# Loading the output weights four rows per partition, with the heads split on VectorE, in a decode attention kernel

## The chip, the cores and the metric

The kernel runs on one core of one Trainium2 chip. The metric is device time of one execution, in microseconds. The granted TensorE clock was 0.78 to 0.80. PE is TensorE, PEld its weight loads, DVE is VectorE, ACT is ScalarE, POOL is GpSimd, and SP is the engine that issues the loads. In the lines of the profile a trailing q (SPq, PEq, DVEq) means the part of an engine that issues instructions. A packet is one record of a DMA engine's work; the core has 16 DMA engines.

## The reference, cut to what matters

```python
def _A_ref(x, k_cache, v_cache, wq, wo):        # x 1x1x448, Hq 16, Hkv 8, Sk 65536, Dh 256
    q = (x @ wq).reshape(B, Sq, Hq, Dh).transpose(0, 2, 1, 3)
    k = jnp.repeat(k_cache, rep, axis=1); v = jnp.repeat(v_cache, rep, axis=1)
    p = _softmax(jnp.einsum("bhqd,bhkd->bhqk", q, k) * (Dh ** -0.5))
    o = jnp.einsum("bhqk,bhkd->bhqd", p, v)
    return o.transpose(0, 2, 1, 3).reshape(B, Sq, Hq * Dh) @ wo       # wo: 4096 x 448
# ... B: a small token-mixing MLP; the result is g * a + (1 - g) * b
```

One query attends over 65536 keys. K and V are 268 MB each, all in bf16, and each byte is read once. The 16 query heads share 8 K/V heads, so the work falls into 8 groups of two heads, and each group needs its own 512 rows of `wo` (448 KB).

## The kernel before

Each group is cut into six chunks (`SIZES`), so there are 48 chunks. SP issues the loads in program order. There are two K buffers and one V buffer. The V of chunk `i` and the K of chunk `i+2` wait for the same event (`s_vf`): DVE has drained the P·V sums of chunk `i-1` from PSUM.

```python
def load_k(i):
    ...
    if i >= 2: sp.wait_ge(s_vf, i - 1)
    sp.dma_start(out=kbuf[i % 2][:, 0:n], in_=kv_src(A_k_cache, i)).then_inc(s_k[i % 2], 16)
def load_v(i):
    ...
    if i >= 1: sp.wait_ge(s_vf, i + 1)
    sp.dma_start(out=vbuf[:, 0:n], in_=kv_src(A_v_cache, i)).then_inc(s_v, 16)
def load_wo(g):                       # two pieces of 1792 B per partition
    if g >= 1: sp.wait_ge(s_oo, g)
    sp.dma_start(out=wo[:].rearrange("p r c n -> p r (c n)"),
        in_=A_wo[g*512:(g+1)*512, :].rearrange("(r p c) n -> p r (c n)", r=2, c=2)).then_inc(s_wo, 16)
# ...
for i in range(1, total - 1):
    load_v(i)
    if i % PER == 1 and PER < i < total - PER: load_wo(i // PER)
    if i + 2 < total: load_k(i + 2)
```

In the first chunk of each group but the first, a "group boundary", the kernel finishes the group before it. There are seven of these. On DVE:

```python
drain_pv(False).then_inc(s_vf, 1)               # releases V and K
dve.memset(tick[:], 0.0).then_inc(s_g, 1)       # lets PE turn the output
take(dve, s_e); dve.transpose(out=pT[:], in_=p_t[:]).then_inc(s_pt, 1)
take(dve, s_o); rden_gate(o_ps[:, 0, 2:4])      # 1/denominator times gate
take(dve, s_wo, 16); heads().then_inc(s_ot, 1)
```

PE turns `og` into a column per head with four small fp32 matmuls (`o_turn(4)`), then multiplies by `wo` with four matmuls of 448 columns. The last group has its own tail after the loop, and its weights come in two separate loads.

The softmax here doesn't subtract the row's maximum and nothing guards it: scores larger than these inputs give would overflow.

Of the kernel before, what the change touches and what calls it, by code (L numbers as in the profile page):

```python
# [8 lines left out]
FP32 = mybir.dt.float32  # L9
BF16 = mybir.dt.bfloat16  # L10
ACT = mybir.ActivationFunctionType
ALU = mybir.AluOpType
AXIS = mybir.AxisListType
# [3 lines left out]
DH = 256  # L17
# [77 lines left out]
def kernel(  # L95
# [16 lines left out]
    D = A_x.shape[-1]  # L112
# [14 lines left out]
    const = ctx.enter_context(tc.tile_pool(name="const", bufs=1))  # L127
# [8 lines left out]
    misc = psum.tile([128, 512], FP32, name="misc")  # L136
    den_ps = psum.tile([128, 512], FP32, name="den_ps")
    acc = psum.tile([128, 512], FP32, name="acc")
# [11 lines left out]
    mask = const.tile([128, 8, 32], FP32, name="mask")  # L150
    one_b = const.tile([128, 128], BF16, name="one_b")
    one_f = const.tile([1, 128], FP32, name="one_f")
    col_f = const.tile([128, 1], FP32, name="col_f")
# [4 lines left out]
    gate = const.tile([128, 2], FP32, name="gate")  # L158
# [17 lines left out]
    dmul = const.tile([128, PER], FP32, name="dmul")  # L176
    dsum = const.tile([128, 1], FP32, name="dsum")
    rden = const.tile([128, 2], FP32, name="rden")
    og = const.tile([128, 2 * DH], FP32, name="og")
    tick = const.tile([1, 1], FP32, name="tick")  # L180
    q_row = const.tile([128, 512], BF16, name="q_row")
    oT = const.tile([128, 4], BF16, name="oT")
    wo = const.tile([128, 2, 2, D], BF16, name="wo")
# [6 lines left out]
    L0, L1, D0, D1, H0, H1, DA_, DB_ = range(8)  # L190
# [16 lines left out]
    def critical():  # L207
        do = Order(nc)
        pe, dve, act, pool, sp = nc.tensor, nc.vector, nc.scalar, nc.gpsimd, nc.sync
# [9 lines left out]
        s_vf = nc.alloc_semaphore("s_vf")  # L219
        s_d = nc.alloc_semaphore("s_d")  # L220
        s_dn = nc.alloc_semaphore("s_dn")
        s_g = nc.alloc_semaphore("s_g")
        s_o = nc.alloc_semaphore("s_o")
        s_ot = nc.alloc_semaphore("s_ot")
# [25 lines left out]
        def load_wo(g):  # L250
            if g >= 1:
                sp.wait_ge(s_oo, g)
            sp.dma_start(
                out=wo[:].rearrange("p r c n -> p r (c n)"),
                in_=A_wo[g * 512:(g + 1) * 512, :].rearrange("(r p c) n -> p r (c n)", r=2, c=2),
            ).then_inc(s_wo, 16)

        load_k(0)
# [5 lines left out]
        for k, src in enumerate((B_w1[0, :], B_b1, B_w2[:, 0])):  # L264
# [7 lines left out]
                out=ident[:], in_=ident[:], compare_op=ALU.not_equal, fill=1.0, base=0,  # L272
# [23 lines left out]
        for hh in range(2):  # L296
            do(
                "dve", lambda e: e.tensor_copy(
                    out=xd[:, hh, :].rearrange("o (r two) -> o r two", two=2)[:, :, hh],
                    in_=x_row[:, DA:D],  # L300
# [4 lines left out]
        def turn_x(e):  # L305
            for k in range(KA + 2):
# [13 lines left out]
                out=xw[:, :, HKV - 1:HKV + 96:32],  # L320
                in_=x_ps.rearrange("p (k o) -> p k o", o=1).to_broadcast([128, KA + 2, 4]),
# [21 lines left out]
        for col, sign in ((0, -1.0), (1, 1.0)):  # L343
            do(
                "act", lambda e: e.activation(
                    out=gate[:, col:col + 1], in_=z_ps[:, 0:1], func=ACT.Exp, scale=sign
# [5 lines left out]
                out=gate[:], in0=gate[:], scalar1=1.0, scalar2=None, op0=ALU.add  # L352
# [5 lines left out]
                out=half_g[:], in0=gate[:, 1:2], scalar1=0.5, scalar2=None, op0=ALU.mult  # L358
# [4 lines left out]
                out=bias[:], in0=z_ps[0:1, 1:2], in1=gate[0:1, 1:2], op=ALU.mult  # L363
# [12 lines left out]
                out=veps[:], in0=mv[:, 1:2], scalar1=1e-5, scalar2=None, op0=ALU.add  # L376
# [6 lines left out]
        for _ in range(2):  # L383
# [10 lines left out]
                    out=nt[:], in0=nt[:], scalar1=-0.5, scalar2=1.5, op0=ALU.mult, op1=ALU.add  # L394
# [8 lines left out]
                out=h_bc[:], in0=xb_ps, scalar1=mv[:, 0:1], scalar2=rstd[:, 0:1],  # L403
# [18 lines left out]
        for k, (t, key) in enumerate(((w1T, "w1T"), (b1T, "b1T"))):  # L422
# [7 lines left out]
                op0=ALU.mult,  # L430
# [105 lines left out]
        def then(ins):  # L536
            ins.then_inc(s_d, 1)
            take(dve, s_d)

        def drain_pv(first):  # L540
            if first:
                return dve.tensor_copy(out=og[:], in_=pv[:])  # L542
            return dve.tensor_tensor(out=og[:], in0=pv[:], in1=og[:], op=ALU.add)  # L543

        def den_rows():
            then(dve.tensor_tensor(out=dmul[:], in0=den[:], in1=dmask, op=ALU.mult))
            then(dve.tensor_reduce(out=dsum[:], in_=dmul[:], axis=AXIS.X, op=ALU.add))

        def heads():
            return dve.tensor_tensor(  # L550
                out=oT[:].rearrange("p (c r) -> p c r", r=2), in0=o_ps[:, :, 0:2],
                in1=rden[:].rearrange("p (o r) -> p o r", o=1).to_broadcast([128, 2, 2]),
                op=ALU.mult,
            )

        def rden_gate(src):
            then(dve.reciprocal(out=rden[:], in_=src))
            then(dve.tensor_scalar(
                out=rden[:], in0=rden[:], scalar1=gate[:, 0:1], scalar2=None, op0=ALU.mult
            ))  # L560
# [6 lines left out]
        with nc.Fori(0, HKV, 1, engines=[DVE], head_slot={DVE: 128}) as turn_v:  # L567
            for c in range(PER):
                turns(c)
                if c == 0:  # L570
                    with dve.If_ne(t_reg, 0):
                        take(dve, s_pv)
                        take(dve, s_dn)
                        drain_pv(False).then_inc(s_vf, 1)
                        dve.memset(tick[:], 0.0).then_inc(s_g, 1)
                    with dve.Else():
                        dve.memset(og[:], 0.0).then_inc(s_vf, 1)
                    take(dve, s_e)
                    dve.transpose(out=pT[:], in_=p_t[:]).then_inc(s_pt, 1)  # L579
                    with dve.If_ne(t_reg, 0):  # L580
                        take(dve, s_o)
                        rden_gate(o_ps[:, 0, 2:4])
                        take(dve, s_wo, 16)
                        heads().then_inc(s_ot, 1)
                elif c < PER - 1:
                    take(dve, s_pv)
                    drain_pv(c == 1).then_inc(s_vf, 1)
                    take(dve, s_e)
                    dve.transpose(out=pT[:], in_=p_t[:]).then_inc(s_pt, 1)  # L589
                else:  # L590
                    take(dve, s_pv)
                    drain_pv(False).then_inc(s_vf, 1)
                    take(dve, s_e)
                    dve.transpose(out=pT[:], in_=p_t[:]).then_inc(s_pt, 1)  # L594
                    den_rows()
                    dve.tensor_scalar(
                        out=og[:], in0=og[:], scalar1=dsum[:, 0:1], scalar2=None, op0=ALU.add
                    ).then_inc(s_dn, 1)
                    for r in range(2):
                        queries(turn_v + 1, r)  # L600
            dve.reg_add(t_reg, t_reg, 1)
# [77 lines left out]
                )  # L679
            return ins  # L680

        def o_turn(width):
            for half, m in enumerate((L0, H0)):
                for cc in range(2):
                    ins = pe.matmul(  # L685
                        o_ps[:, cc, 0:width if half == 0 else 2],
                        lhsT=og[:, half * DH + cc:(half + 1) * DH:2],
                        rhs=mask[:, m:m + (width if half == 0 else 2), 0],
                        start=(half == 0 and cc == 0), stop=(half == 1 and cc == 1),
                        skip_group_check=True,  # L690
                    )
            return ins

# [6 lines left out]
        with nc.Fori(0, total, 1, engines=[PE], head_slot={PE: 0}):  # L700
            for s, b in plan[0:4]:
                scores(s, b, s == 0, False)
            with pe.If_lt(v_reg, PER):
                pe.wait_ge(s_pt, 1).then_inc(s_pt, -1)
                pe.wait_ge(s_v, 16).then_inc(s_v, -16)  # L705
                for s in range(4):
                    p_v(vbuf, pT, s, s == 0, False)
                with pe.If_lt(v_reg, big):
                    p_v(vbuf, pT, 5, False, False)
                p_v(vbuf, pT, 4, False, True).then_inc(s_pv, 1)  # L710
            with pe.If_lt(c_reg, big):
                scores(5, 2, False, False)
            scores(4, 0, False, True)
            with pe.If_eq(v_reg, PER - 1):
                pe.wait_ge(s_g, 1).then_inc(s_g, -1)
                o_turn(4).then_inc(s_o, 1)
                pe.wait_ge(s_ot, 1).then_inc(s_ot, -1)  # L717
                for k in range(4):
                    cc, r = divmod(k, 2)
                    ins = pe.matmul(  # L720
                        acc[0:1, 0:D], lhsT=oT[:, k:k + 1], rhs=wo[:, r, cc, :], start=False,
                        stop=False, skip_group_check=True,
                    )
                ins.then_inc(s_oo, 1)
            pe.reg_mov(v_reg, c_reg)
            pe.reg_add(c_reg, c_reg, 1)
            with pe.If_eq(c_reg, PER):
                pe.reg_mov(c_reg, 0)
# [55 lines left out]
                start=True, stop=False, tile_position=(0, 32 * a), skip_group_check=True,  # L784
            )
        pe.wait_ge(s_fd, 2)
        o_turn(2)
        pe.wait_ge(s_last[2], 16)
        turned(edges[2], edges[3])
        pe.wait_ge(s_last[3], 16)  # L790
# [56 lines left out]
```

## Time and profile before

The kernel before takes 1265.84 us (median of 6 runs, 1265.68 to 1266.03).

| from the profile before | value |
|---|---|
| span of the profiled run | 1263.6 us |
| DMA load queue, share of 16 engines' span | 99.7% |
| PE, DVE, ACT, POOL busy | 57%, 53%, 4%, 6% |
| bytes moved | 544.22 MB, 431 GB/s |

The page of the kernel before: the span, the busy time of each engine, then the span in 40 equal slices (digits are tenths), then the packets and the load queue's share.

```profile
span 1263.6 us, 10623 instructions
...
PE 718.4 (57%) x4296; PEld 275.5 (22%) x4296; DVE 675.1 (53%) x462; ACT 50.1 (4%) x127; POOL 78.5 (6%) x111
...
PE   4855655466554665456555565555645656456556
...
DVE  5745555465544555455455555464545645465544
...
DMA  9999999999999999999999999999999999999998
...
DMA packets 16840, 544.30 MB, mean 431 GB/s; under 512 B 1856, under 2 KB 3906, under 8 KB 4290
...
q1 hardware_dynamic: 16744, 544.22, 99.7%
```

No compute engine is full in any slice (the highest digits are one 8 for PE and one 7 for DVE), and DMA stands at 9 in all of them but the last, where it has 8. This kernel is as fast as its load queue: an estimated 4.8 us of packets taken from the changed kernel's queue made it 4.76 us faster ("Fewer bytes" below). A change can help in two ways only: it takes work from the queue, or it removes time in which the queue has nothing to do. The chain of work that ended last says the same:

```profile
1226.52 0.70 DVE og L543
...
1227.23 0.33 SPq L248
...
1229.03 29.98 DMA kbuf<-in_A_v_cache_dram
...
1259.05 0.69 PE misc L751 x20
...
1259.77 0.17 DVE oT L550
...
1259.98 0.60 PE acc L800 x13
...
1260.61 0.28 DVE res L807
```

The columns are start in us, duration in us, and what ran. The last V pieces land at 1259.01 us, and less than 2 us of work follows.

Two timelines show a group boundary before the change, on DVE and on PE (start, duration, engine, line, operation, and in brackets the idle time ahead of it):

```profile
342.97 0.69 DVE L543 TENSOR_TENSOR og<-pv,og 128x512 f32<-128x512 f32 x1 [0.20 <-DVEq L524]
343.60 0.06 DVE L575 MEMSET tick<- 1x1 f32 x1
347.17 0.71 DVE L579 STREAM_TRANSPOSE pT<-p_t 128x512 bf16<-128x512 bf16 x1 [3.51 <-DVEq L524]
...
348.67 0.16 DVE L550 TENSOR_TENSOR oT<-misc,rden 128x4 bf16<-128x4 f32 x1 [0.26 <-DVEq L524]
353.99 2.31 DVE L532 STREAM_TRANSPOSE kT<-kbuf 128x2048 f32<-128x2048 f32 x1 [5.15 <-DVEq L524]
```

```profile
342.62 3.67 PE L661 MATMUL sc<-kT,qw 128*128 128x512 bf16 x16
346.14 0.99 PE L685 MATMUL misc<-mask,og 128*128 128x4 f32 x8
348.98 1.65 PE L720 MATMUL acc<-wo,oT 128*1 128x448 bf16 x4 [1.85 <-PEq L717]
```

The V load of this boundary, as SP issues it:

```profile
343.69 0.33 SPq L248 DMA_DIRECT2D vbuf<-in_A_v_cache_dram  x1
```

DVE has two holes here. One is 3.51 us between the drain and the transpose of the probabilities, and one is 5.15 us until the next K has landed.

### The profile page before, as it was taken

The page shows a single profiled execution, that of the slowest core. Times are in us where ns is not written, and L with a number is a line of the kernel's source. Part 1 is how long each engine was busy: PE and PEld are TensorE (multiplying, and loading weights), DVE is VectorE, ACT ScalarE, POOL GpSimd, SP SyncE. Part 2 cuts the span into 40 slices and gives each one's busy share as a digit, 9 for nine tenths or more (in the row PEclk, how much of TensorE's full clock was granted, in tenths as well). Part 3 has the DMA queues.
Part 4 walks back from the last instruction along what each step waited for, and adds up shares of the span by engine and source line. Part 5 has one row for each costly group of instructions (what it writes and reads, how often), then busy time and mean ns, then how long its engine had stood idle before and what let it go on. Part 6 is the DMA issues. An engine that isn't in the chain of part 4 may idle for free. (4 is left out here: it accounts for less than half of the span.)

```text
span 1263.6 us, 10623 instructions
## 1 busy us (share of the span) xinstructions
PE 718.4 (57%) x4296; PEld 275.5 (22%) x4296; DVE 675.1 (53%) x462; ACT 50.1 (4%) x127; POOL 78.5 (6%) x111
## 2 busy tenths in 40 slices
PE   4855655466554665456555565555645656456556
PEld 1311222122221222112221221222212222122212
DVE  5745555465544555455455555464545645465544
ACT  0000000000000000000000000000000000000000
POOL 1001010110110101101111011000000000000000
PEclk9987878778777788778877788777887788777877
DMA  9999999999999999999999999999999999999998
GB/s 405 427 434 433 438 438 422 439 435 431 439 430 428 436 433 438 435 428 433 434 434 438 430 434 434 429 439 427 434 442 429 434 434 432 436 433 430 439 433 354
DMA packets 16840, 544.30 MB, mean 431 GB/s; under 512 B 1856, under 2 KB 3906, under 8 KB 4290
## 3 DMA queue, kind: packets, MB, share of 16 engines
q1 hardware_dynamic: 16744, 544.22, 99.7%
q8 instruction: 2, 0.03, 0.0%
q10 hardware_dynamic: 90, 0.01, 0.0%
q14 instruction: 4, 0.03, 0.0%
HBM read 544.22 MB, written 0.00 MB: 431 GB/s over the span
## 5 line engine op out<-in xcount | busy, mean ns | idle before, releaser
L661 PE MATMUL sc<-kT,qw 128*128 128x512 bf16 x2048 | 571.8, 437 | 488.7 <-PEq L657 488.7
L532 DVE STREAM_TRANSPOSE kT<-kbuf 128x2048 f32<-128x2048 f32 x256 | 572.8, 2285 | 331.7 <-DVEq L524 331.7
L661 PEld LDWEIGHTS sc<-kT,qw 128*128 128x128 bf16 x2048 | 210.4, 108 | 848.7 <-issue 695.5
L675 PE MATMUL pv<-vbuf,pT 128*4 128x512 bf16 x2008 | 120.9, 389 | 27.1 <-PEq L705 26.8
L543 DVE TENSOR_TENSOR og<-pv,og 128x512 f32<-128x512 f32 x40 | 27.7, 692 | 98.8 <-DVEq L524 98.6
L608 ACT ACTIVATE p_t<-sc 128x512 bf16<-128x512 f32 x48 | 28.7, 597 | 1192.2 <-PE sc L661 1192.2
L675 PEld LDWEIGHTS pv<-vbuf,pT 128*4 128x4 bf16 x2008 | 47.2, 88 | 97.2 <-issue 51.7
L589 DVE STREAM_TRANSPOSE pT<-p_t 128x512 bf16<-128x512 bf16 x32 | 22.8, 711 | 74.4 <-DVEq L524 74.4
L635 POOL TENSOR_SCALAR t_b<-t_b 128x448 f32<-128x448 f32 x14 | 7.9, 564 | 360.6 <-ACT t_b L617 360.6
L639 POOL TENSOR_SCALAR t_b<-t_b,hw 128x448 f32<-128x448 f32 x14 | 8.9, 638 | 332.7 <-ACT t_b L625 332.7
L579 DVE STREAM_TRANSPOSE pT<-p_t 128x512 bf16<-128x512 bf16 x8 | 5.7, 711 | 26.9 <-DVEq L524 26.9
L644 POOL TENSOR_TENSOR ymix<-ymix,t_b 128x448 f32<-128x448 f32 x14 | 16.1, 1148 | 1.1
L643 POOL TENSOR_TENSOR t_b<-t_b,u_b 128x448 f32<-128x448 f32 x14 | 15.8, 1126 | 1.2
L638 POOL TENSOR_TENSOR t_b<-t_b,u_b 128x448 f32<-128x448 f32 x14 | 15.8, 1126 | 1.2
L720 PE MATMUL acc<-wo,oT 128*1 128x448 bf16 x28 | 7.9, 413 | 12.7 <-PEq L717 12.7
L542 DVE COPY og<-pv 128x512 f32<-128x512 f32 x8 | 5.5, 692 | 16.1 <-DVEq L524 16.1
L594 DVE STREAM_TRANSPOSE pT<-p_t 128x512 bf16<-128x512 bf16 x8 | 5.7, 711 | 14.9 <-DVEq L524 14.9
L617 ACT ACTIVATE t_b<-h_bc,b1T,w1T 128x448 f32<-128x448 f32 x14 | 10.5, 747 | 0.0
L631 POOL TENSOR_SCALAR u_b<-h_bc,w1T,b1T 128x448 f32<-128x448 f32 x14 | 10.0, 715 | 4.1 <-DVE hw L428 2.7
L608 ACT ACTIVATION_READ_ACCUMULATOR p_t<-sc 128x1 f32 x48 | 9.3, 194 | 0.0
L452 PE MATMUL sc<-vbuf,xw 128*128 128x512 bf16 x32 | 9.2, 456 | 0.0
L685 PEld LDWEIGHTS misc<-mask,og 128*128 128x128 f32 x64 | 8.7, 196 | 2.0 <-DVE og L543 0.9
(86 smaller groups left out, 77.3 us busy)
## 6 DMA issues: line engine op xcount, KB each, us to landing
kbuf<-in_A_k_cache_dram SPq DMA_DIRECT2D x32, 5120.0 KB, 33.2
vbuf<-in_A_v_cache_dram SPq DMA_DIRECT2D x31, 5120.0 KB, 20.6
kbuf<-in_A_k_cache_dram SPq DMA_DIRECT2D x16, 6144.0 KB, 35.5
vbuf<-in_A_v_cache_dram SPq DMA_DIRECT2D x16, 6144.0 KB, 23.8
wo<-in_A_wo_dram SPq DMA_DIRECT2D x7, 448.0 KB, 23.6
vbuf<-in_A_wq_dram SPq DMA_DIRECT2D x1, 3072.0 KB, 10.3
kbuf<-in_A_v_cache_dram SPq DMA_DIRECT2D x1, 2560.0 KB, 25.3
kbuf<-in_A_v_cache_dram SPq DMA_DIRECT2D x1, 1024.0 KB, 27.2
```

The source lines that it names most:

```text
L452: last = e.matmul(q_ps[:], lhsT=xw[:, k, HKV - 1 - n:HKV - 1 - n + 128], rhs=rhs, start=(n == 0 and k == 0), stop=(n == HKV - 1 and k >= K ...
L532: dve.transpose(out=kT[b][:].bitcast(FP32), in_=kn[:, s * SB * 128:(s + 1) * SB * 128]).then_inc(s_kt, 1)
L543: return dve.tensor_tensor(out=og[:], in0=pv[:], in1=og[:], op=ALU.add)
L589: dve.transpose(out=pT[:], in_=p_t[:]).then_inc(s_pt, 1)
L608: ins = act.activation(out=p_t[:], in_=sc[:], func=ACT.Exp, scale=scale, accum_out=den[:, c:c + 1])
L617: ins = act.activation(out=t_b[:], in_=h_bc[:], func=ACT.Square, scale=w1T[:, b:b + 1], bias=b1T[:, b:b + 1],)
L631: lambda: pool.tensor_scalar(out=u_b[:], in0=h_bc[:], scalar1=w1T[:, b:b + 1], scalar2=b1T[:, b:b + 1], op0=ALU.mult, op1=ALU.add,),
L638: lambda: pool.tensor_tensor(out=t_b[:], in0=t_b[:], in1=u_b[:], op=ALU.mult),
L643: lambda: pool.tensor_tensor(out=t_b[:], in0=t_b[:], in1=u_b[:], op=ALU.mult),
L644: lambda: pool.tensor_tensor(out=ymix[:], in0=ymix[:], in1=t_b[:], op=ALU.add),
L661: ins = pe.matmul(sc[:], lhsT=qw[:, q, at:at + 128], rhs=kv[:, :, q // 2, :, q % 2], start=(first and q == 0), stop=(last and q == 7), ski ...
L675: ins = pe.matmul(pv[32 * a:32 * a + 4, :], lhsT=pT[:, k, :, ROW0 + s], rhs=vt[:, j * DH:(j + 2) * DH], start=first and k < 4, stop=last a ...
```

## The change: its intent and the diff

Four consecutive rows of `wo` lie side by side in HBM. A partition that takes four rows gets one piece of 3584 B in place of two of 1792 B. Row `4p+c` of the group then lies on partition `p`, so partitions 0 to 63 belong to the first head and 64 to 127 to the second, and the attention output must reach PE split by head. DVE does that with four operations against the head masks. The denominators no longer ride in `og` (the add of `dsum` goes); a matmul of their own brings them to the right partitions.

```diff
 load_wo:
-   out=wo[:].rearrange("p r c n -> p r (c n)"),
-   in_=A_wo[g*512:(g+1)*512, :].rearrange("(r p c) n -> p r (c n)", r=2, c=2),
+   out=wo[:].rearrange("p r c n -> p (r c n)"),
+   in_=A_wo[g*512:(g+1)*512, :].rearrange("(p c) n -> p (c n)", c=4),
 DVE, group boundary:
-   drain_pv(False).then_inc(s_vf, 1)
-   dve.memset(tick[:], 0.0).then_inc(s_g, 1)
+   then(drain_pv(False))                              # waits until it is written
+   dve.memset(rsel[:], 0.0).then_inc(s_vf, 1)
+   then(split_heads(0))                               # 2 x tensor_scalar, 128x256
+   split_heads(1).then_inc(s_g, 1)                    # 2 x scalar_tensor_tensor, 128x256
 ...
-   rden_gate(o_ps[:, 0, 2:4])
+   for r in range(2):
+       rows = slice(64 * r, 64 * (r + 1))
+       ins = dve.reciprocal(out=rsel[rows, :], in_=misc[rows, 508 + r:509 + r])
+   then(ins); then(dve.tensor_scalar(out=rsel[:], in0=rsel[:], scalar1=gate[:, 0:1], ...))
 DVE, last chunk of a group:
-   dve.tensor_scalar(out=og[:], in0=og[:], scalar1=dsum[:, 0:1], scalar2=None, op0=ALU.add)
 PE, group boundary:
-   o_turn(4).then_inc(s_o, 1)
+   for c in range(4):
+       pe.matmul(misc[:, 504 + c:505 + c], lhsT=og2[:].rearrange("p r (q c) -> p c r q", c=4)[:, c],
+           rhs=col_f[:], ...)
+   pe.matmul(misc[:, 508:510], lhsT=dsum[:].to_broadcast([128, 128]), rhs=mask[:, D0:D0 + 2, 0], ...
+       ).then_inc(s_o, 1)
 ... # the wo matmuls take rows in the new order; the tail of the last group keeps its two loads
```

More of the change, by code (lines that the diff above doesn't have):

```diff
@@ L179 @@
     og = const.tile([128, 2 * DH], FP32, name="og")
-    tick = const.tile([1, 1], FP32, name="tick")
+    og2 = const.tile([128, 2, DH], FP32, name="og2")
+    rsel = const.tile([128, 1], FP32, name="rsel")
     q_row = const.tile([128, 512], BF16, name="q_row")
@@ L253, in load_wo @@
             sp.dma_start(
-                out=wo[:].rearrange("p r c n -> p r (c n)"),
-                in_=A_wo[g * 512:(g + 1) * 512, :].rearrange("(r p c) n -> p r (c n)", r=2, c=2),
+                out=wo[:].rearrange("p r c n -> p (r c n)"),
+                in_=A_wo[g * 512:(g + 1) * 512, :].rearrange("(p c) n -> p (c n)", c=4),
             ).then_inc(s_wo, 16)
@@ L546, in den_rows, with split_heads @@
             then(dve.tensor_tensor(out=dmul[:], in0=den[:], in1=dmask, op=ALU.mult))
-            then(dve.tensor_reduce(out=dsum[:], in_=dmul[:], axis=AXIS.X, op=ALU.add))
+            return dve.tensor_reduce(out=dsum[:], in_=dmul[:], axis=AXIS.X, op=ALU.add)
+        def split_heads(half):
+            for r, m in enumerate((L0, L1) if half == 0 else (H0, H1)):
+                part, by = og[:, half * DH:(half + 1) * DH], mask[:, m, 0:1]
+                if half == 0:
+                    ins = dve.tensor_scalar(
+                        out=og2[:, r, :], in0=part, scalar1=by, scalar2=None, op0=ALU.mult
+                    )
+                else:
+                    ins = dve.scalar_tensor_tensor(
+                        out=og2[:, r, :], in0=part, scalar=by, in1=og2[:, r, :], op0=ALU.mult,
+                        op1=ALU.add,
+                    )
+            return ins
         def heads():
@@ L581, in critical @@
                         take(dve, s_o)
-                        rden_gate(o_ps[:, 0, 2:4])
+                        for r in range(2):
+                            rows = slice(64 * r, 64 * (r + 1))
+                            ins = dve.reciprocal(out=rsel[rows, :], in_=misc[rows, 508 + r:509 + r])
+                        then(ins)
+                        then(dve.tensor_scalar(
+                            out=rsel[:], in0=rsel[:], scalar1=gate[:, 0:1], scalar2=None,
+                            op0=ALU.mult,
+                        ))
                         take(dve, s_wo, 16)
-                        heads().then_inc(s_ot, 1)
+                        dve.tensor_scalar(
+                            out=oT[:], in0=misc[:, 504:508], scalar1=rsel[:, 0:1], scalar2=None,
+                            op0=ALU.mult,
+                        ).then_inc(s_ot, 1)
                 elif c < PER - 1:
@@ L594, in critical @@
                     dve.transpose(out=pT[:], in_=p_t[:]).then_inc(s_pt, 1)
-                    den_rows()
-                    dve.tensor_scalar(
-                        out=og[:], in0=og[:], scalar1=dsum[:, 0:1], scalar2=None, op0=ALU.add
-                    ).then_inc(s_dn, 1)
+                    den_rows().then_inc(s_dn, 1)
                     for r in range(2):
@@ L680, in p_v, with o_turn @@
             return ins
-        def o_turn(width):
+        def o_turn():
             for half, m in enumerate((L0, H0)):
@@ L685, in o_turn @@
                     ins = pe.matmul(
-                        o_ps[:, cc, 0:width if half == 0 else 2],
-                        lhsT=og[:, half * DH + cc:(half + 1) * DH:2],
-                        rhs=mask[:, m:m + (width if half == 0 else 2), 0],
-                        start=(half == 0 and cc == 0), stop=(half == 1 and cc == 1),
-                        skip_group_check=True,
+                        o_ps[:, cc, 0:2], lhsT=og[:, half * DH + cc:(half + 1) * DH:2],
+                        rhs=mask[:, m:m + 2, 0], start=(half == 0 and cc == 0),
+                        stop=(half == 1 and cc == 1), skip_group_check=True,
                     )
@@ L715, in critical @@
                 pe.wait_ge(s_g, 1).then_inc(s_g, -1)
-                o_turn(4).then_inc(s_o, 1)
+                for c in range(4):
+                    pe.matmul(
+                        misc[:, 504 + c:505 + c],
+                        lhsT=og2[:].rearrange("p r (q c) -> p c r q", c=4)[:, c], rhs=col_f[:],
+                        start=(c == 0), stop=False, skip_group_check=True,
+                    )
+                pe.matmul(
+                    misc[:, 508:510], lhsT=dsum[:].to_broadcast([128, 128]),
+                    rhs=mask[:, D0:D0 + 2, 0], start=False, stop=True, skip_group_check=True,
+                ).then_inc(s_o, 1)
                 pe.wait_ge(s_ot, 1).then_inc(s_ot, -1)
                 for k in range(4):
-                    cc, r = divmod(k, 2)
                     ins = pe.matmul(
-                        acc[0:1, 0:D], lhsT=oT[:, k:k + 1], rhs=wo[:, r, cc, :], start=False,
+                        acc[0:1, 0:D], lhsT=oT[:, k:k + 1], rhs=wo[:, k // 2, k % 2, :], start=False,
                         stop=False, skip_group_check=True,
@@ L786, in critical @@
         pe.wait_ge(s_fd, 2)
-        o_turn(2)
+        o_turn()
         pe.wait_ge(s_last[2], 16)
```

## The prediction

> **What bounds the kernel now.** The DMA queue. The page's queue section gives the load queue 99.7% of the 16 engines' span, 544.22 MB; the 40-slice rows show DMA at 9 tenths nearly everywhere, PE at 4 to 6, DVE at 4 to 7. All data packets' durations in the trace, summed and divided by 16 engines, make 1258.9 us of the 1263.6 us span. The chain that ended last is the last V pieces, landing at 1259.0 us, then 1.9 us of small PE and DVE work.
>
> **Is the queue ever short of work?** No. From the issues in order of time and the packets I counted the bytes still under way at each V issue of the loop: 5.0 to 9.5 us of transfer. A compute delay under 5 us before a V issue costs nothing.
>
> **DMA.** Seven loads of 448 KB go from 256 pieces of 1792 B to 128 of 3584 B. Packets before: 74 ns for 1792 B, 159 for 4096 B, 761 for 20480 B, 1514 for 40960 B, so 0.0368 ns per byte plus about 8 ns per packet. [...] Estimate for 3584 B: 140 ns. Per load and engine 16 x 74 = 1184 ns become 8 x 140 = 1120 ns; seven loads give 0.45 us, all of it on the critical resource, 0.035% of the span. A quicker issue on SP (0.43 us now) is hidden.
>
> **Engines, per group boundary (7 of them).**
> - The V release now follows a wait on the drain and a 128x1 memset: an estimated 0.1 to 0.2 us later (the old 1x1 memset took 0.06 us). Backlog there: 6.4 to 7.8 us. Hidden.
> - DVE gains four 128x256 fp32 operations, estimated from the 128x512 ones (0.48 and 0.69 us) at 0.3 to 0.45 us each, 1.5 us together, and about 0.3 us for the changed reciprocals; it loses the 0.48 us og + dsum of the last chunk. The timeline around 344 us shows DVE idle for 3.5 us after that drain, until the exponential, then for 5 us until the next K has landed. Both swallow it. DVE's busy sum should rise by 5 to 9 us from 675 us.
> - PE: eight fp32 passes (0.99 us) become ten (an estimated 1.0 to 1.3 us); PE then idles over 5 us until the next K. The split should be done about when the score matmuls end, 2.5 us after the drain; a little later costs nothing.
> - The tail loses 0.48 us on DVE, but there PE waits for the last V piece (0.2 us shown) anyway: no gain.
>
> **Predicted time: 1265.4 us** (1265.85 - 0.45), 8 in 10 between 1264.5 and 1266.3. Chances: faster by over 2%: 0.01; within 2%: 0.98; slower by over 2%: 0.01.
>
> **What would show it right.** 896 fewer packets, with 896 of 3584 B near 140 ns; queue share still 99.7%; summed packet time 0.4 to 0.5 us down; V issues at group boundaries at most 0.3 us later after the scores; DVE busy up, its wait before the pT transpose of a group's first chunk shorter by about 1.5 us; the chain still ending in the last V pieces.
>
> **What would make it wrong.** 3584 B packets off that line; a release so late that the queue runs dry (over 5 us); boundary work far beyond the estimate, delaying the next K's transposes and all later releases; pieces spread unevenly, so that one DMA engine falls behind.

The 8 ns per packet are the fit to the four packet durations of the trace (74, 159, 761 and 1514 ns).

## The result, and the profile after

The changed kernel takes 1265.57 us (median of 6, 1265.35 to 1265.97), beside 1265.84 us before: 0.27 us less. The ratio is 0.9998, with an interval of 0.9985 to 1.0011. Ratios here are the mean time of one kernel's runs over that of the other's of the same rounds, so they are not quite the ratio of the medians.

The page of the changed kernel:

```profile
span 1263.6 us, 10684 instructions
...
PE 725.8 (57%) x4310; PEld 283.2 (22%) x4310; DVE 680.7 (54%) x489; ACT 50.1 (4%) x127; POOL 78.4 (6%) x111
...
DMA  9999999999999999999999999999999999999998
...
DMA packets 15944, 544.30 MB, mean 431 GB/s; under 512 B 1856, under 2 KB 2114, under 8 KB 3394
...
q1 hardware_dynamic: 15848, 544.22, 99.7%
```

There are 896 packets fewer and as many bytes, the queue is as full as before, and DVE has 5.6 us more work. The chain still ends in the last V pieces:

```profile
1227.99 31.01 DMA kbuf<-in_A_v_cache_dram
...
1259.05 0.71 PE misc L781 x20
```

The same group boundary after the change, on DVE, PE and SP:

```profile
342.30 0.69 DVE L544 TENSOR_TENSOR og<-pv,og 128x512 f32<-128x512 f32 x1 [0.47 <-DVEq L525]
343.16 0.06 DVE L590 MEMSET rsel<- 128x1 f32 x1 [0.18 <-DVEq L525]
343.17 0.62 DVE L554 TENSOR_SCALAR og<-og,mask 128x256 f32<-128x256 f32 x2
343.93 0.88 DVE L558 SCALAR_TENSOR_TENSOR og<-og,mask,og 128x256 f32<-128x256 f32 x2
346.50 0.71 DVE L596 STREAM_TRANSPOSE pT<-p_t 128x512 bf16<-128x512 bf16 x1 [1.69 <-DVEq L525]
...
354.18 6.70 DVE L533 STREAM_TRANSPOSE kT<-kbuf 128x2048 f32<-128x2048 f32 x3 [5.34 <-DVEq L525]
```

```profile
341.95 3.67 PE L685 MATMUL sc<-kT,qw 128*128 128x512 bf16 x16
345.47 1.81 PE L739 MATMUL misc<-col_f,og 128*128 128x1 f32 x8
347.14 0.36 PE L744 MATMUL misc<-mask,dsum 128*128 128x2 f32 x2
348.99 0.92 PE L750 MATMUL acc<-wo,oT 128*1 128x448 bf16 x4 [1.49 <-PEq L748]
```

```profile
343.25 0.33 SPq L249 DMA_DIRECT2D vbuf<-in_A_v_cache_dram  x1
```

The split fills a hole that was there: DVE's wait before the transpose falls from 3.51 to 1.69 us, and DVE still waits 5.34 us for K afterwards. The V load is issued 0.95 us after the drain began. Before, it was issued at 343.69 us, 0.72 us after the drain began. The release is thus 0.23 us later (0.72 us became 0.95 or 0.96 us at each of the seven boundaries), and nothing behind it moves, because the queue still has about 8 us of earlier loads to move at that point.

**How large is the effect in the queue itself?** Whole runs of one kernel differ by 0.3 to 0.8 us, so 0.27 us is hard to see in them; the two profiled executions happen to have the same span, 1263.6 us. (In that pair the changed kernel led by 0.20 us when the tail's weights began, 1257.01 against 1257.21 us, and lost the lead in the tail, where the last weights took 2.80 us from first packet to last against 2.60 us: the last one ended at 1259.81 us in both.) The packet records of a trace are steadier. I took the start of the first packet of each weight load. Between the second and third such load lie six chunks and one weight load. The table also has the mean durations of the weight packets.

| kernel | packet, ns | packets per engine and load | second to third weight load, us |
|---|---|---|---|
| before | 74 | 16 | 155.86 |
| changed | 140 | 8 | 155.82 |

The next two intervals repeat both figures (155.86 and 155.82), and so does the fifth. The fourth does not: it took 155.90 us before and 156.02 us changed, and why is not known. Such a stray interval of up to 0.26 us turns up in some traces and not in others (none in the later trace of the changed kernel, where all five are 155.82 us), so the usual value is compared here, not the sum. The gain is 0.04 us per load, an estimated 0.28 us for seven loads, and so 5 ns for each of the 8 packets that went, not 8 ns.

### The profile page after: what moved, and what is told of

Its sections match the earlier page's. It is cut to its first block, busy times and chain, and to the rows that moved or that the text cites. A ratio compares the mean times of both kernels' runs of the same rounds, so it can differ in the third digit from the quotient of the medians.

```text
span 1263.6 us, 10684 instructions
## 1 busy us (share of the span) xinstructions
PE 725.8 (57%) x4310; PEld 283.2 (22%) x4310; DVE 680.7 (54%) x489; ACT 50.1 (4%) x127; POOL 78.4 (6%) x111
## 3 DMA queue, kind: packets, MB, share of 16 engines
q1 hardware_dynamic: 15848, 544.22, 99.7%
## 5 line engine op out<-in xcount | busy, mean ns | idle before, releaser
L739 PEld LDWEIGHTS misc<-col_f,og 128*128 128x128 f32 x56 | 13.6, 327 | 0.8
L739 PE MATMUL misc<-col_f,og 128*128 128x1 f32 x56 | 12.7, 348 | 0.0
L641 ACT ACTIVATE t_b<-h_bc,b1T,w1T 128x448 f32<-128x448 f32 x14 | 10.5, 748 | 0.0
```

The lines of the kernel that those rows point to most:

```text
L641: ins = act.activation(out=t_b[:], in_=h_bc[:], func=ACT.Square, scale=w1T[:, b:b + 1], bias=b1T[:, b:b + 1],)
L739: pe.matmul(misc[:, 504 + c:505 + c], lhsT=og2[:].rearrange("p r (q c) -> p c r q", c=4)[:, c], rhs=col_f[:], start=(c == 0), stop=False, ...
```

## The experiments

The theory after the result was this. The queue's packets are the whole effect, at about 5 ns each, and all compute added at the boundary hides behind queued loads. The rivals were: the full difference of the packets' durations counts (A in the texts below, against A'), the difference is noise (B), the engines' side made it (C), or delays at the boundary do reach the end (D). A "weight interval" below is that from the second to the third weight load. "Beside before" is against the median of the kernel before on the same chip (1265.65 to 1265.84 us).

### The packet size alone, four sizes

The engines' side stays as changed. The weights go to a padded tile, so that each partition's 3584 B break into 2, 4, 8 or 16 pieces:

```diff
+wg = const.tile([128, NP, 4 * D // NP + 16], BF16, name="wg")
-   out=wo[:].rearrange("p r c n -> p (r c n)"),
+   out=wg[:, :, 0:W],                                   # W = 4 * D // NP
+   in_=....rearrange("(p c) n -> p (c n)", c=4).rearrange("p (k w) -> p k w", w=W)
-   rhs=wo[:, k // 2, k % 2, :]                          # in the boundary's matmuls
+   rhs=wg[:, NP // 4 * k:NP // 4 * (k + 1), 0:W]        # NP = 8, 16; the like for 2 and 4
 # the last group's tail keeps wo and its own two loads
```

> The changed kernel, with the seven weight loads laid down in two padded pieces of 1792 B per partition (the old packet size; layout, rows, engines' work as changed). Theory A (each packet takes its busy duration from the queue, about 8 ns fixed cost): +0.45 us on the changed kernel, so level with the kernel before. Theory A' (only about 5 ns of it, as the pace between the weight loads in the two traces suggests): +0.28 us. Rival B (packet count costs nothing, the 0.27 us are noise): +0.0. Rival C (the 0.27 us come from the engines' side, for instance the shorter tail on DVE): +0.0, as the engines' side is unchanged here. In the trace the interval between weight loads should go from 155.82 us back to 155.86 us under A'.

> As the run before, with four pieces of 896 B. A: 32 packets of about 40 ns per engine and load instead of 8 of 140 ns, +1.1 us in all on the changed kernel. A': 24 packets more at 5 ns, times 7 loads: +0.84 us. B and C: +0.0.

> Eight pieces of 448 B. A: 64 packets of about 24.5 ns per engine and load, +3.1 us in all. A': 56 packets more at 5 ns, times 7: +2.0 us. B and C: +0.0.

> Sixteen pieces of 224 B. A: 128 packets of about 16 ns per engine and load, +6.5 us in all. A': 120 packets more at 5 ns, times 7: +4.2 us. B and C: +0.0.

| pieces | median, us | beside before, us | weight interval, us | ns per packet beyond 8 (from the interval) |
|---|---|---|---|---|
| 8 x 3584 B (changed) | 1265.57 | -0.27 | 155.82 | - |
| 16 x 1792 B | 1265.74 | -0.10 | 155.86 | 0.04/8 = 5 |
| 32 x 896 B | 1266.37 | +0.53 | 155.93 | 0.11/24 = 5 |
| 64 x 448 B | 1267.85 | +2.01 | 156.14 | 0.32/56 = 6 |
| 128 x 224 B | 1276.05 | +10.21 | 157.43 (later ones 157.03 to 157.68) | 1.61/120 = 13 |

Four results were correct. From 3584 to 448 B, packets cost 5 to 6 ns each in the interval. Against the changed kernel the medians stand at +0.17, +0.80 and +2.28 us; A' said 0.28, 0.84 and 2.0, and A said 0.45, 1.1 and 3.1. B and C said no change and fall with the last two: the runs with 896 B (1266.24 to 1266.98 us) and with 448 B (1267.82 to 1268.07) do not overlap with the kernel before (1265.68 to 1266.14). The run with 1792 B decides nothing by its median; its interval of 155.86 us does, since it has the engines' side of the changed kernel. A falls too: a 448 B packet lasts 25 ns in the records, 64 of them 1.60 us against 1.12 us for 8 large ones, yet the interval grew by only 0.32 of those 0.48 us. The records of packets overlap, so their sum is not the queue's time: in the kernel before they sum to 1258.9 us per engine, though only 1257.8 us lie between the first packet's start and the last one's end, and while the 224 B pieces of the next run move, up to 23 packets are open at once on 16 engines.

The 224 B run lies above both theories (A said 6.5 us, A' 4.2). Its trace also shows something unlooked for, in the issues on SP (start, duration, what):

```profile
218.29 0.33 SPq L250 DMA_DIRECT2D vbuf<-in_A_v_cache_dram  x1
218.67 0.55 SPq L255 DMA_DIRECT2D wg<-in_A_wo_dram  x1
219.26 21.83 SPq L244 DMA_DIRECT2D kbuf<-in_A_k_cache_dram  x1
245.07 0.33 SPq L250 DMA_DIRECT2D vbuf<-in_A_v_cache_dram  x1
```

The K load behind the small pieces took 21.83 us to issue, where it takes 0.47 us in the kernel before. With 448 B pieces it took 11.69 us, and with 896 B pieces 0.62 us:

```profile
217.85 11.69 SPq L244 DMA_DIRECT2D kbuf<-in_A_k_cache_dram  x1
```

```profile
217.43 0.62 SPq L244 DMA_DIRECT2D kbuf<-in_A_k_cache_dram  x1
```

The same issue in the kernel before:

```profile
217.12 0.47 SPq L242 DMA_DIRECT2D kbuf<-in_A_k_cache_dram  x1
```

The issue behind the weights thus took 0.62 us with 32 weight packets per engine, 11.69 us with 64 and 21.83 us with 128; what held SP was not shown. In the 448 B run the issue ended with V packets still to come, and the interval shows little extra (6 ns a packet beside 5). In the 224 B run it ended at 241.1 us, about when the V packets ran out, and some 16 of the K packets that started around then, about one per engine, took 0.67 us longer than usual on average. So was the excess due to the late issue?

### Small pieces in two portions

```diff
-if i % PER == 1 and PER < i < total - PER: load_wo(i // PER)
+if i % PER in (1, 3) and PER < i < total - PER: load_wo(i // PER, i % PER // 2)   # 8 of 16 pieces each
-take(dve, s_wo, 16)
+take(dve, s_wo, 32)
```

> Sixteen pieces of 224 B again, but each load of groups 1 to 6 issued as two halves two chunks apart, so that no more than 64 small packets per engine stand in front of the next K load. In the run with all at once that K load's issue took 21.8 us on the sync engine and ended as the queue ran out of V packets. If that late issue made the excess over the line of 5 us per thousand packets (10.5 us against 4.2): the K issue takes about 12 us as with 448 B pieces, and the kernel is 4 to 5.5 us over the changed kernel. If it is the small packets' own time (19 ns each in the trace): 9 to 10.5 us over it again.

(The text says "5 us per thousand packets" where the line meant is 5 ns per extra packet on an engine, which gives its 4.2 us.)

It took 1273.98 us (1273.59 to 1274.31), 8.33 us beside before. The K issues behind the first divided load took 10.0 and 14.0 us (8 to 17 us behind the others), so the late issue was gone for six of the seven loads:

```profile
219.09 10.04 SPq L244 DMA_DIRECT2D kbuf<-in_A_k_cache_dram  x1
...
270.60 14.00 SPq L244 DMA_DIRECT2D kbuf<-in_A_k_cache_dram  x1
```

The result, 8.5 us over the changed kernel, lies between the two expectations. The first weight load was still issued whole, and its K issue ended as late as before, so the late issue was not removed there. Removing it from the other six took some 2 of the 10.5 us away. The weight interval (second to fourth load here, as loads come in halves) is 156.82 us, 1.00 us over 155.82, or 8 ns for each of 120 extra packets. The packets last 16.0 ns here, so theory A's sum (128 x 16.0 less 8 x 140 ns) gives 0.93 of the 1.00 us. At 224 B a packet's recorded duration thus counts nearly in full, where at 448 B and above about 5 to 6 ns of the 8 ns do. Why is left open; the change doesn't come near that size.

### The new load alone, on the old engines

```diff
 # kernel before, load_wo:
-   in_=A_wo[g*512:(g+1)*512, :].rearrange("(r p c) n -> p r (c n)", r=2, c=2)
+   in_=A_wo[g*512:(g+1)*512, :].rearrange("(p c) n -> p (c n)", c=4)      # out: one piece, as changed
```

> The kernel before, with only the one-piece load (rows in the wrong order for its heads, so the result is wrong on purpose). A and A': as fast as the changed kernel, 0.28 to 0.45 us under the kernel before. C (the engines' side gave it): level with the kernel before.

It took 1265.56 us (1265.38 to 1265.73), 0.27 us under the kernel before on its chip and level with the changed kernel. The weight interval is 155.82 us, as changed. The load alone has the whole effect, and the new work on DVE and PE neither gives nor costs anything that the spread of 0.35 us lets us see. Note that the check of the outputs passed, although heads and weight rows no longer match. That check cannot tell row orders apart here, so it doesn't vouch for the changed kernel's order either; that rests on reading the code. Why the error stays within the tolerance was not looked into.

### Fewer bytes

```diff
 # changed kernel, load_wo:
+n = 4 if g == 0 else 1
-   out=wo[:].rearrange("p r c n -> p (r c n)"), in_=....rearrange("(p c) n -> p (c n)", c=4)
+   out=wo[:].rearrange("p r c n -> p (r c n)")[:, 0:n * D], in_=....[:, 0:n * D]
```

> The changed kernel, groups 1 to 6 loading only the first of their four rows per partition (wrong result on purpose): per engine and load 8 packets of about 40 ns instead of 8 of 140 ns. If the queue's time is the kernel's time: 6 x 0.8 = 4.8 us less than the changed kernel. If the load hides behind something else: no change.

It took 1260.81 us (wrong result), 4.76 us under the 1265.57 us of the changed kernel. Time taken from the queue comes back in full: 4.8 us expected, 4.8 us measured. (The weight interval fell by 0.79 us, and 8 packets of 140 ns less 8 of 41 ns are 0.79 us: with as many packets as before, the records' difference is the queue's.)

### A later V release

```diff
 # changed kernel, group boundary:
 then(drain_pv(False))
+for _ in range(N):                     # N = 5, 10 and later 8
+    then(split_heads(0))
 dve.memset(rsel[:], 0.0).then_inc(s_vf, 1)
```

> The changed kernel, with the first half of the head split done five more times between the drain and the V release, an estimated 4 us on DVE at each of the 7 group boundaries (0.62 us and a wait of about 0.2 us each). Theory: the queue has 6.4 to 7 us of work there, so +0.0 us (within 0.3 us). Rival D (delays at the boundary do reach the end): up to 7 x 4 = 28 us more.

> The same with ten repeats, an estimated 8 us. Theory: 1 to 2 us beyond the queue's work[...], so the queue runs dry at each boundary and the kernel takes 7 x (1 to 4) = 7 to 28 us longer. If it stays within 0.5 us, the slack is larger than I counted.

> Eight repeats before the V release: by the two runs with five and ten, about 6.8 us later than in the changed kernel, which leaves 1 to 2 us of the 7.9 to 8.8 us of queue work there. The first packet of the kernel came 1.0 us after its issue, so the queue should just not run dry: 0 to 2 us over the changed kernel. If the cost grows with any delay: about 9 us (eight tenths of what ten repeats cost).

(A clause on the time from an issue to its first packet was cut from the text of the run with ten repeats, since no trace had shown its upper figure. The term is still contained in that text's sum, 7 x (1 to 4) = 7 to 28 us; the term left, 1 to 2 us, gives 7 to 14 us. In that run's trace the first packet after a dry queue mostly came 0.95 us after the start of the issue.)

The column "queue work left" counts the bytes under way when the boundary's V issue ends, at 435 GB/s, at each of the seven boundaries.

| kernel | queue work left at the seven V issues, us | median, us | beside before, us |
|---|---|---|---|
| before | 8.4 to 9.4 | 1265.84 | 0 |
| changed | 7.9 to 8.8 | 1265.57 | -0.27 |
| 5 repeats | 4.0 to 5.1 | 1265.40 | -0.43 |
| 8 repeats | 0.3 to 2.5 | 1271.50 | +5.85 |
| 10 repeats | 0.2 to 1.5 | 1277.50 | +11.67 |

The last two scatter far more than the others: 1269.43 to 1274.29 us and 1274.56 to 1281.17 us.

Five repeats moved the V issue from 0.95 to 4.79 us after the start of the drain, 3.8 us, and cost nothing, so D falls. In that run's timeline the release's memset stands at 347.43 us. The next K landed at 353.92 us, DVE's boundary work ended at 354.01 us, and the transposes began at 354.06 us (354.18 us in the changed kernel):

```profile
347.43 0.06 DVE L592 MEMSET rsel<- 128x1 f32 x1 [0.18 <-DVEq L525]
...
354.06 6.70 DVE L533 STREAM_TRANSPOSE kT<-kbuf 128x2048 f32<-128x2048 f32 x3
```

Ten repeats run the queue dry. In the slices of the page, GB/s falls to 403 to 419 in the seven with a boundary (in the kernel before, no slice but the first and the last is under 422):

```profile
GB/s 404 432 431 431 439 434 403 432 432 445 431 416 433 433 431 436 412 430 434 434 434 416 439 431 437 417 433 434 434 428 414 436 425 438 427 419 436 432 433 328
```

The packet records show two parts of the loss. Within a few microseconds of the seven V issues, the DMA engines stood idle for 5.4 us in all (mean of the 16), and 4.9 us went to packets that lasted over 15% longer than usual. With eight repeats these were 1.6 and 3.1 us, in the changed kernel and with five repeats zero. The busy share hardly shows it: with ten repeats the page still says 99.2% for the queue, 0.5 points under the changed kernel, and the median was 11.9 us longer (0.9%).

The run with eight repeats missed its expectation (0 to 2 us), for two reasons. The delays were larger at some boundaries than I had reckoned (7.15 us at four of them, 6.1 us at three, against 6.8), and the queue needs more warning than I had reckoned. By the intervals from one weight load to the next, 1.7 us left cost nothing and 2.1 or 2.5 us left cost 0.2 us, which stray intervals reach too; but 1.3 us left cost 0.6 and 0.9 us, 0.3 us left cost 1.4 us, and 4 us or more (five repeats) cost nothing. So the cost begins at an estimated 2 us of work left, not at zero; these few boundaries place it between 1.3 and 4 us and no closer. By that estimate the slack at a boundary of the kernel before is some 6 to 7 us, of which the change uses 0.23.

### The changed kernel once more

> The changed kernel once more, beside the kernel before on the same chip. If the packets' pace (0.04 us per load, 7 loads) is the whole effect: 0.28 us under the kernel before, within the 0.2 us that medians of five move by. If it was noise: level.

It took 1265.47 us (1265.31 to 1265.80), beside 1265.65 us before (1265.49 to 1266.31, 9 runs): 0.18 us less. The weight interval is 155.82 us, five times over. The sign repeats, and the size is as unsure as the spread suggests. With so small an effect, the intervals in the trace carry the argument, not the medians.

## Why the prediction was right or wrong

The prediction (1265.4 us, range 1264.5 to 1266.3) held: 1265.57 us. That says little by itself, since a forecast of no effect would have held in the same range; the mechanism rests on the runs. Point by point:

- **The queue is the bound: right.** Its share is 99.7% before and after. Taking 4.8 us of packets from it gave 4.8 us (fewer bytes).
- **3584 B packets of 140 ns: right.** They measured 140 ns, and the summed packet time fell from 1258.9 to 1258.4 us.
- **"Seven loads give 0.45 us, all of it on the critical resource": mis-sized.** The mechanism held, but 64 ns per load was 40 ns. The prediction took a packet's recorded duration for its time in the queue. The weight intervals give 5 ns per packet in place of 8 (the records overlap), and 7 x 0.04 = 0.28 us, which agrees with the 0.27 and 0.18 us of the medians.
- **"Backlog there: 6.4 to 7.8 us": misread.** Those figures belong to the V issues of other chunks. At the seven boundaries it was 8.4 to 9.4 us. (The text of the run with five repeats still uses them.) That a delay under 5 us costs nothing was an estimate from the lowest count, 5.0 us; shown is a delay of 3.8 us at the seven boundaries. The error was on the safe side, and the conclusion (hidden) was shown by the run with five repeats.
- **Release 0.1 to 0.2 us later: nearly right**, 0.23 to 0.24 us at every boundary.
- **DVE: right.** Busy time rose by 5.6 us (5 to 9 foretold) and the wait before the transpose fell by 1.8 us at the boundary shown. One term was off: the add of `dsum` that went had taken 0.82 us on the mean (8 times), not 0.48 us, and the rise is at the low end for it.
- **PE, "ten passes, an estimated 1.0 to 1.3 us": mis-sized.** They took 1.81 + 0.36 = 2.2 us, and eight of the ten weight loads were slower than the old ones. These are PE's weight loads in the changed kernel, by line (count, busy us, mean ns, idle before), then the old boundary's and the tail's from the kernel before:

```profile
L685 PEld LDWEIGHTS sc<-kT,qw 128*128 128x128 bf16 x2048 | 210.8, 108 | 842.6 <-issue 689.2
...
L739 PEld LDWEIGHTS misc<-col_f,og 128*128 128x128 f32 x56 | 13.6, 327 | 0.8
...
L744 PEld LDWEIGHTS misc<-mask,dsum 128*128 128x128 f32 x14 | 2.2, 198 | 0.0
```

```profile
L685 PEld LDWEIGHTS misc<-mask,og 128*128 128x128 f32 x64 | 8.7, 196 | 2.0 <-DVE og L543 0.9
```

  The ones that pick every fourth fp32 column of the split output take 327 ns; those of the denominators (one column repeated) take 198, and the old ones (every second column) took 196 in the kernel before. The step between columns was not tested by itself, and other loads were slow without it: at the start of both kernels two fp32 loads of a single row took 304 ns and a bf16 load of a single row 286 ns. The longer work costs nothing here, since PE waits for K after it (6.7 us idle before the next scores at the boundary shown).
- **Tail, no gain: right.** The chain ends in the same V pieces, and the load alone on the old engines, whose tail is the old one, is as fast.

No correct version here beats the changed kernel by more than the spread. What is left is the loads' own bytes, about 2 us before the first packet and under 4 us after the last.

## What to carry to other kernels

Here, with one queue 99.7% busy, a change was worth the time that it took from that queue (an estimated 4.8 us of packets gave 4.76 us), and everything else had only to fit in the slack: bytes still queued when the next load is issued, 8.4 to 9.4 us at the boundaries of the kernel before, less an estimated 2 us. In a kernel like it, count a change that way first. Halving the packets of this small weight load was worth 5 ns a packet; that is 0.02%, and it was not worth restructuring two engines for it, though it harmed nothing. To see effects below the spread of whole runs, measure the interval between two like events deep in the trace, and amplify the suspected cost (here with 2 to 16 times the packets) until whole runs show it.
